# Window attention ahead of two MoE layers: finer steps in the attention's order of issue (key loads apart from query loads, the two shifted copies of the values apart, the softmax of a unit in two halves)

## The chip, the cores and the metric

The kernel runs on one core of a Trainium2 chip. The core has TensorE (PE in the profile; its weight loads are PEld), VectorE (DVE), ScalarE (ACT), GpSimd (POOL) and SyncE (SP), which issues the DMAs of this kernel. Each engine takes its instructions in the order in which the program gives them. The metric is the device time of the one launch, in microseconds.

## The reference

For 4 batches and 8 heads of width 64 there are 512 local tokens and 32 global ones. A local query sees the 32 global keys and the local keys within 32 positions; a global query sees all 544. The result, 2,176 tokens of 512 numbers, goes through two MoE-like layers.

```
s_g = scale * q_g @ k_all.T;  out_g = softmax(s_g) @ v_all
s_ll = where(|i - j| <= 32, scale * q_l @ k_l.T, -1e9)
s_lg = scale * q_l @ k_g.T
out_l = softmax([s_lg, s_ll]) @ [v_g, v_l]
x = concat([out_g, out_l]) as (2176, 512)
h = x @ w1_in;  x = (h * tanh(softplus(h))) @ w1_out
h = x @ w2_in;  y = (h * cos(h)) @ w2_out
```

## The kernel before

The launch has two parts. In the first the attention runs, interleaved with the first work of the first layer; in the second the two layers run, bound by matrix products whose operands are split into a high and a low half.

The attention is cut into 16 pairs of heads (4 a batch) and 32 units, two to a pair. The string ORDER holds all its steps in the order in which they are written into the program, as `name:number`, with an ending `a` or `d` where a copy may go to ScalarE or to VectorE. A step is one Python function that emits instructions for one engine or several. Since every engine is in order, ORDER fixes each engine's own queue, and the DMA queue of SyncE too; how the engines stand against each other is left to the waits. ORDER2 does the same for the second layer.

For a pair `pp`: `lq` loads queries and keys (four DMAs of 128 KB, `qn` and `kn`, two buffers each), `Q` and `K` transpose them on TensorE (L525, L539), `q`, `k`, `k2`, `h` copy them to `QT` and to the windowed keys `kw`, `kg` adds the global keys. For each unit `u`, `S` makes 16 score products (L563) in two of three PSUM buffers `s`; `X` masks and finds the maximum of each of four blocks on VectorE (L579) and exponentiates each on ScalarE (L582); `ne` (POOL, L587), `ni` (DVE), `N` (POOL, L595) normalise; `TA` transposes the probabilities (L606) and `ta` copies them; `NB`, `TB`, `tb` do so for the global keys' part. `lv` loads the values twice, shifted by 32 tokens down (`ve`) and up (`vo`), three buffers each; `lw` overwrites a few rows of `ve` with the global values, so it waits for `lv`'s landing; `vg` loads the global values of a batch. `AV` is the product with the values (L627, L633), `av` its copy into `xT`. The global queries go by pairs of pairs: `lg`, `G`, `g` prepare them, `SG` scores, `sm`, `st`, `se` (an exponential on ScalarE that reads an `s` buffer), `ss`, `si`, `sn` make the softmax, `TG`, `tg` transpose and copy, `AG` and `ag` make and copy the product (L705, L709). PSUM tiles of the transposes and of `AG` and `L` rotate through three buffers.

Between them stand the first layer's steps: `c0` loads 512 KB of weights into one of two buffers `cs` (L209), `c1` and `c5` (ScalarE) and `c2`, `d2`, `c3`, `d3`, `e3`, `c4`, `d5` (VectorE) turn one unit of double-precision weights into a high and a low half, for units 0 to 8; `xs` splits a piece of `xT`, `L` is a first-layer product of 12 matmuls (L795 to L797), `lh` copies it. `ff:0` and `ff:1` run the first group of the second part ahead. After ORDER's last step the second part goes on with the weight conversion, at one or two units a group of products, and with the products themselves (L795 to L797, L1118).

Of the kernel before, what the change touches and what calls it, by code (L numbers as in the profile page):

```python
# [32 lines left out]
    sn:0d N:2 S:4 Q:3 q:3a lv:0 tb:0d kg:3 X:4 TG:0 ni:3 lw:0 S:5 tg:0d TA:2 ne:4 lq:4 AG:0 NB:1 SG:1 X:5 S:6 d2:0  # L33
    ta:2d vg:0 lv:1 c1:0 sm:1 st:1 ag:0 se:1 N:3 ne:5 ni:4 c3:0 TA:3 ni:5 K:4 TB:1 AV:0 ta:3a X:6 ss:1 lw:1 d3:0
    e3:0 G:1 k2:4a N:4 ne:6 k:4d h:4d NB:2 tb:1a S:7 lv:2 si:1 N:5 av:0d AG:1 xs:0a AV:1 lq:5 g:1 TA:4 ni:6 X:7
    c4:0 Q:4 ta:4a ag:1 Q:5 av:1d q:4a N:6 ne:7 K:5 q:5a TA:5 sn:1a ni:7 k:5d kg:4 k2:5d TA:6 ta:5a S:8 c0:1 h:5d
    ta:6a TB:2 N:7 c2:1 tb:2a NB:3 lg:2 TA:7 TB:3 lw:2 G:2 c5:0 ta:7a X:8 S:9 lq:6 tb:3d TG:1 g:2 kg:5 X:9 tg:1d
    SG:2 AV:2 S:10 Q:6 lq:7 ne:8 K:6 sm:2 st:2 ne:9 lv:3 av:2d c1:1 se:2 ni:8 ni:9 NB:4 K:7 X:10 lw:3 S:11 k:6a
    k:7a k2:6d lq:8 ss:2 q:6d lv:4 d2:1 si:2 h:6a k2:7d N:8 kg:6 AV:3 h:7a AG:2 AG:3 ne:10 TA:8 vg:1 X:11 ag:2
    sn:2d ta:8a ag:3 Q:7 lw:4 c3:1 TG:2 q:7a lq:9 S:12 TB:4 N:9 xs:1d d3:1 ni:10 kg:7 xs:2a tg:2d ne:11 lv:5 tb:4a  # L40
    TA:9 av:3d ta:9a K:8 lw:5 X:12 SG:3 e3:1 S:13 N:10 k:8d ne:12 ni:11 k2:8a AG:4 NB:5 AV:4 sm:3 st:3 se:3 X:13
    N:11 ag:4 S:14 h:8d TB:5 av:4d TA:10 ni:12 TA:11 ss:3 ta:10a tb:5d si:3 ta:11a kg:8 Q:8 q:8a K:9 lv:6 X:14 N:12
    ne:13 TA:12 ni:13 S:15 c4:1 NB:6 ta:12d k2:9d k:9a AV:5 h:9a lq:10 lw:6 N:13 AG:5 TB:6 kg:9 X:15 TA:13 ne:14
    av:5d tb:6a ni:14 S:16 lg:3 sn:3d lv:7 ag:5 ne:15 ni:15 ta:13a X:16 TG:3 Q:9 S:17 tg:3d q:9d NB:7 N:14 TA:14
# [86 lines left out]
def kernel(  # L131
# [14 lines left out]
    nc = tc.nc  # L146
# [1103 lines left out]
```

## Time and profile before

| | us |
|---|---|
| median of 3 runs (lowest, highest) | 885.45 (883.87, 886.25) |
| profiled execution: time of its own | 883.55 |
| its span, first to last instruction | 881.8 |
| TensorE busy, of the span | 860.8 (98%) |
| VectorE busy | 738.2 (84%) |
| ScalarE busy | 483.3 (55%) |
| start of the first second-part product (L1118) | 163.76 |

Times in rows are from the span's start. A matmul's shown duration overlaps with the next one's, so TensorE's work is read from the distance between starts, not from durations.

### The profile page before, as it was taken

What the parts mean: (1) busy time and instruction counts of PE and PEld (TensorE: products, weight loads), DVE (VectorE), ACT (ScalarE), POOL (GpSimd) and SP (SyncE); (2) the same over time, 40 slices, a digit from 0 to 9 for tenths busy, and PEclk for the clock granted to TensorE, in tenths of its full rate; (3) what the DMA queues carried; (4) which work ended last, traced back from release to release, by engine and by line L of the source; (5) the groups of instructions that cost most, each with busy time, mean ns of one, the idle gap of its engine ahead of it and who ended that gap; (6) DMA issues with size and microseconds to landing.
All of it is one profiled execution on the core that took longest, in us unless ns stands there. A gap on an engine that the chain in (4) does not pass through costs nothing.

```text
span 881.8 us, 16128 instructions
## 1 busy us (share of the span) xinstructions
PE 860.8 (98%) x5995; PEld 790.4 (90%) x5995; DVE 738.2 (84%) x1513; ACT 483.3 (55%) x948; POOL 85.9 (10%) x137
## 2 busy tenths in 40 slices
PE   7999999999998999999999999999999999999998
PEld 5677888999998999999999998899888888889886
DVE  5989888798889889999989589889776777787786
ACT  6878875674564334444344347566455554545554
POOL 3565565000000000000000000000000000000000
PEclk9999999999999999999999999999999999999999
DMA  7977762156677899887765995724648209025011
GB/s 161 198 158 161 168 152 74 49 156 215 233 252 266 328 338 361 286 294 237 277 243 193 387 414 220 283 90 148 234 144 321 109 14 355 1 79 202 1 60 72
DMA packets 133886, 174.98 MB, mean 198 GB/s; under 512 B 77872, under 2 KB 100400, under 8 KB 133808
## 3 DMA queue, kind: packets, MB, share of 16 engines
q1 hardware_dynamic: 133808, 173.95, 59.8%
q8 instruction: 48, 0.79, 0.4%
q14 instruction: 30, 0.25, 0.1%
HBM read 115.59 MB, written 58.33 MB: 197 GB/s over the span
## 4 chain that ended last, share of the span: by engine, by line
PE 76%; DMA 10%; DVE 8%; ACT 3%; issue 2%; SPq 0%; POOL 0%; DVEq 0%; ACTq 0%; POOLq 0%
PE acc L1019 17%; PE acc L1118 14%; PE h L1050 13%; PE acc L1050 7%; PE h L795 5%; PE h L797 5%; PE h L796 5%; DMA cs<-in_moe_w_out_dram 4%; DMA cs<-in_moe_w_in_dram 2%; PE s L563 2%; PE av L633 1%; DVE ca L237 1%; DMA op<-stage 1%; PE ta L606 1%; DVE x L772 1%
## 5 line engine op out<-in xcount | busy, mean ns | idle before, releaser
L1118 PE MATMUL acc<-gh,w 128*128 128x384 f32 (+1 forms) x768 | 187.9, 328 | 0.0
L1118 PEld LDWEIGHTS acc<-gh,w 128*128 128x128 f32 x768 | 136.2, 189 | 0.0
L1118 PE MATMUL acc<-gl,w 128*128 128x384 f32 (+1 forms) x384 | 126.2, 329 | 2.9 <-DVE x L868 1.9
L795 PE MATMUL h<-x,w 128*128 128x384 f32 (+1 forms) x384 | 126.1, 328 | 0.6 <-DVE x L772 0.5
L797 PE MATMUL h<-x,w 128*128 128x384 f32 (+1 forms) x384 | 125.2, 326 | 0.0
L796 PE MATMUL h<-x,w 128*128 128x384 f32 (+1 forms) x384 | 125.1, 326 | 0.0
L1050 PE MATMUL h<-w,gh 128*128 128x512 f32 x352 | 109.8, 393 | 0.0
L1019 PE MATMUL acc<-xo,w 128*128 128x384 f32 (+1 forms) x402 | 76.4, 327 | 1.6 <-DVE hs L1041 1.6
L1050 PEld LDWEIGHTS h<-w,gh 128*128 128x128 f32 x352 | 66.1, 188 | 11.8
L1118 PEld LDWEIGHTS acc<-gl,w 128*128 128x128 f32 x384 | 72.6, 189 | 4.2 <-DVE x L868 2.2
L1019 PEld LDWEIGHTS acc<-xo,w 128*128 128x128 f32 x402 | 68.0, 188 | 6.6 <-DVE hs L1041 2.8
L841 ACT ACTIVATE w<-w 128x768 f32<-128x768 f32 (+2 forms) x50 | 39.0, 780 | 63.5 <-DVE w L838 63.5
L795 PEld LDWEIGHTS h<-x,w 128*128 128x128 f32 x384 | 72.1, 188 | 1.5 <-issue 0.8
L796 PEld LDWEIGHTS h<-x,w 128*128 128x128 f32 x384 | 72.1, 188 | 0.0
L797 PEld LDWEIGHTS h<-x,w 128*128 128x128 f32 x384 | 72.1, 188 | 0.0
L1050 PE MATMUL h<-w,gl 128*128 128x512 f32 x176 | 69.2, 393 | 2.2 <-DVE part L345 1.0
L1041 DVE TENSOR_TENSOR hs<-u,acc 128x384 f32<-128x384 f32 (+1 forms) x91 | 47.4, 526 | 28.3 <-PE acc L1019 26.9
L831 ACT ACTIVATE k<-hs,magic 128x768 f32<-128x768 f32 (+2 forms) x50 | 43.5, 871 | 49.2 <-DVE w L838 43.1
L1050 PE MATMUL acc<-w,gh 128*128 128x512 f32 x192 | 59.9, 393 | 0.0
L582 ACT ACTIVATE pr<-pr,nm 128x160 f32<-128x160 f32 x128 | 53.2, 421 | 10.6 <-DVE nm L579 10.4
L835 DVE SCALAR_TENSOR_TENSOR w<-k,hs 128x768 f32<-128x768 f32 (+2 forms) x50 | 44.0, 881 | 8.2 <-ACT k L832 6.5
L822 DVE TENSOR_TENSOR gl<-w,gh 128x768 fp32r<-128x768 f32 (+1 forms) x48 | 43.5, 907 | 8.3 <-ACT gh L818 8.3
(179 smaller groups left out, 1783.0 us busy)
## 6 DMA issues: line engine op xcount, KB each, us to landing
w<-scr SPq DMA_DIRECT2D x44, 512.0 KB, 7.0
scr<-co SPq DMA_DIRECT2D x31, 512.0 KB, 3.0
x<-x SPq DMA_DIRECT2D x32, 384.0 KB, 5.9
xo<-op SPq DMA_DIRECT2D x15, 768.0 KB, 5.7
cs<-in_moe_w_in_dram SPq DMA_DIRECT2D x22, 512.0 KB, 4.2
cs<-in_moe_w_out_dram SPq DMA_DIRECT2D x22, 512.0 KB, 4.1
scr<-lab SPq DMA_DIRECT2D x21, 512.0 KB, 3.8
xo<-op SPq DMA_DIRECT2D x10, 640.0 KB, 4.9
```

What stands on the lines that cost most here:

```text
L582: nc.scalar.activation(out=pr[:, i], in_=pr[:, i], func=AF.Exp, bias=nm[:, i:i + 1], scale=-1.0, accum_out=l[:, i:i + 1])
L795: nc.tensor.matmul(ps[:, c, 0:n], wh[:, k, :], xl, start=(k == 0), stop=False)
L796: nc.tensor.matmul(ps[:, c, 0:n], wh[:, k, :], xh, start=False, stop=False)
L797: nc.tensor.matmul(ps[:, c, 0:n], wl[:, k, :], xh, start=False, stop=(k == NK - 1))
L822: nc.vector.tensor_tensor(out=gl, in0=v["w"], in1=gh.bitcast(F32), op=ALU.subtract)
L831: nc.scalar.activation(out=k[:, y], in_=of("h")[:, z], func=AF.Identity, scale=INV2PI, bias=magic[:, 0:1])
L835: nc.vector.scalar_tensor_tensor(out=of("t")[:, z], in0=k[:, y], scalar=-C1, in1=of("h")[:, z], op0=ALU.mult, op1=ALU.add)
L841: nc.scalar.activation(out=of("t")[:, z], in_=of("t")[:, z], func=AF.Sin, scale=0.5)
L1019: nc.tensor.matmul(to, l[:, i + c], r, start=c == 0 and m == 0, stop=c == 1 and m == 2)
L1041: nc.vector.tensor_tensor(out=of[out](), in0=of[x](), in1=bank(s, o), op=ALU.add)
L1050: nc.tensor.matmul(singles()[a], l[:, a * P:(a + 1) * P], r, start=(j, c) == (0, 0) and m == 0, stop=(j, c) == (3, 1) and m == 2)
L1118: nc.tensor.matmul(o[:, 0:n], w[:, a * P:(a + 1) * P], r[:, c, :], start=(not goes_on and g == 0 and m == 0), stop=(not stays and g == G - ...
```

## The change

ORDER is replaced by another sequence of 798 steps in place of 722, and some steps are cut in two so that the parts can stand apart in it:

- `lq` loads queries alone and a new `lk` loads keys;
- `lv` loads `ve` alone and a new `lo` loads `vo`;
- `X` handles the first two of a unit's four blocks and a new `Y` the last two;
- `g` copies the global keys, and a new `gz` the global queries; `tg` copies four blocks, and a new `tu` the fifth;
- the copies of `g`, `gz`, `tu` and `ag`, which VectorE always made, can now go to either engine.

The matrix products, the DMAs with their sizes, the softmax instructions and the conversion steps are the same in number and shape. The 32 units, 16 pairs and 9 loads `c0` all stay; ORDER2 stays as it is.

```
 ORDER = """
-    hot:-1 hot:19 lq:0 K:0 lg:0 k:0a Q:0 q:0a k2:0d h:0a G:0 g:0 lq:1 setup lq:2 lg:1 kg:0 S:0 X:0 Q:1 c0:0 K:1
-    k2:1d k:1d h:1a kg:1 S:1 q:1a Q:2 ne:0 X:1 S:2 ne:1 ni:0 q:2a X:2 K:2 c2:0 SG:0 k:2a lq:3 N:0 ni:1 k2:2a sm:0
-    TA:0 S:3 NB:0 N:1 st:0 ta:0a se:0 h:2d K:3 ne:2 ni:2 TB:0 k:3a X:3 TA:1 k2:3d kg:2 ss:0 si:0 ne:3 h:3d ta:1a
...
+    hot:-1 hot:19 lk:0 K:0 lg:0 G:0 k:0a k2:0d lq:0 Q:0 setup lk:1 g:0d h:0d lq:1 kg:0 q:0a lk:2 K:1 k:1a k2:1a
+    h:1a S:0 lg:1 gz:0d X:0 Y:0 Q:1 q:1d S:1 X:1 kg:1 lk:3 Y:1 SG:0 K:2 ne:0 ni:0 sm:0 S:2 N:0 st:0 k2:2a se:0 lq:2
+    X:2 ne:1 ni:1 k:2d TA:0 N:1 K:3 lv:0 ss:0 Y:2 ta:0d S:3 lq:3 k2:3a h:2d si:0 sn:0d Q:2 TA:1 k:3a h:3a X:3 Q:3
+    q:2d lo:0 G:1 ta:1a kg:2 ne:2 ni:2 NB:0 N:2 gz:1a Y:3 ne:3 S:4 q:3d TB:0 tb:0a lv:1 TA:2 kg:3 g:1d lk:4 X:4 Y:4
...
+    vg:2 N:20 TA:19 TG:4 c0:5 ta:19a tg:4a Y:21 c3:4 c2:5 S:22 SG:5 X:22 tu:4d AV:8 lk:12 Y:22 ne:21 AG:8 ni:21
...
+    ag:11a ni:26 d2:6 Y:27 lv:13 S:28 TB:12 tb:12d av:11a c3:6 ne:27 TA:24 TA:25 ta:24a ni:27 kg:15 lw:12 vg:3 N:26
+    lq:15 c5:5 lv:14 ta:25a lo:13 TG:6 X:28 tg:6a xs:10a xs:11d tu:6d d5:5 AV:12 Y:28 SG:7 S:29 d3:6 sm:7 Q:15
+    av:12a st:7 c0:7 L:8 se:7 lh:8a ne:28 X:29 c2:7 L:9 q:15d e3:6 L:10 ss:7 c1:7 d2:7 lh:9d Y:29 NB:13 ni:28 c4:6
...
+    ta:29d AV:14 c0:9 ni:30 c4:7 TG:7 N:30 lh:13a ne:31 ni:31 c5:7 tg:7a d5:6 L:14 ff:1 NB:15 av:14d c2:8 d5:7 N:31
+    L:15 tu:7d TB:15 lh:14a TA:30 tb:15d lh:15a ta:30d TA:31 AG:14 ta:31d ag:14a AV:15 d2:8 av:15d AG:15 ag:15d
 """
-        def load_qk(pp):
+        def load_tokens(pp, n, src):
             b, p = divmod(pp, NPAIR)
-            qk[pp] = []
-            for n, src in (("qn", q_l), ("kn", k_l)):
-                t = ap.tile([P, NJ, 2, D], F32, tag=n, name=n, bufs=2)
-                for h in range(2):
-                    nc.sync.dma_start(out=t[:, :, h, :], in_=src[b, 2 * p + h].rearrange("(c p) d -> p c d", p=P))
-                qk[pp].append(t)
+            t = ap.tile([P, NJ, 2, D], F32, tag=n, name=n, bufs=2)
+            for h in range(2):
+                nc.sync.dma_start(out=t[:, :, h, :], in_=src[b, 2 * p + h].rearrange("(c p) d -> p c d", p=P))
+            return t
...
+        def load_e(pp):
+            load_v(pp, ve, -32)
+
+        def load_o(pp):
+            load_v(pp, vo, 32)
...
+        def g_copy2(b):
             t, z = live["g", b], qz[b % 2]
-            nc.vector.tensor_copy(out=z[0:64, :, 0:SG], in_=t[0:64, :, 0:SG])
-            nc.vector.tensor_copy(out=z[64:128, :, SG:2 * SG], in_=t[64:128, :, 0:SG])
+            copy("gz", b, z[0:64, :, 0:SG], t[0:64, :, 0:SG])
+            copy("gz", b, z[64:128, :, SG:2 * SG], t[64:128, :, 0:SG])
...
-        def s_max(u):
+        def s_max(u, which=(0, 1)):
...
-            for i in range(4):
+            for i in which:
...
+        def tg_copy2(m):
+            copy("tu", m, pg_of(m)[:, NJ], live["tg", m][1])
...
-            nc.vector.tensor_copy(out=xT[:, p, b * S:b * S + SG], in_=live["ag", pp])
+            copy("ag", pp, xT[:, p, b * S:b * S + SG], live["ag", pp])
```

## Rows read from the trace of the kernel before

**Rows 1.** All engines in order of time, where the second part begins.

```profile
163.52 0.85 ACT L818 ACTIVATE gh<-hraw 128x768 fp32r<-128x768 f32 x1 [2.10 <-PE avg L705]
163.76 0.44 PE L1118 MATMUL acc<-gl,w 128*128 128x384 f32 x1 [0.33 <-DVE xT L709]
```

**Rows 2.** The chain that ended last: start, length, what; three of its later pieces.

```profile
167.73 3.64 DMA cs<-in_moe_w_in_dram
...
272.83 6.02 PE acc L1118 x24
...
283.01 4.16 PE acc L1118 x24
```

**Rows 3.** TensorE's wait at 273 us, and a stretch behind it.

```profile
272.83 0.48 PE L1118 MATMUL acc<-gl,w 128*128 128x384 f32 x1 [1.92 <-DVE x L868]
274.00:276.00 2.00, 2.00 (x8) 2.00 (x8) 2.00 (x4) 2.00 (x4) 0.00 (x0) 0.50 1.02 409
```

**Rows 4.** The same chain: one piece for each kind of attention step.

```profile
53.23 0.70 PE s L563 x16
...
54.31 0.44 PE ta L606 x4
...
55.54 0.89 PE sg L650 x4
...
63.97 0.63 PE av L627 x4
64.60 1.08 PE av L633 x32
65.68 0.56 PE avg L705 x20
```

**Rows 5.** Stretches: length, busy PE, PEld, DVE, ACT, POOL (count), clock, DMA.

```profile
20.00:30.00 10.00, 9.34 (x141) 6.35 (x139) 9.89 (x43) 9.63 (x42) 5.33 (x9) 1.00 0.57 129
```

**Rows 6.** All engines in order of time, the head.

```profile
8.12 0.29 DVE L518 COPY qz<-gt 64x128 f32<-64x128 f32 x1
...
9.20 0.77 PE L563 MATMUL s<-kw,QT 64*64 64x160 f32 x16 [1.47 <-DVE kw L534]
...
13.01 0.17 DVE L591 RECIPROCAL r<-l 128x4 f32<-128x4 f32 x1
...
14.75 0.22 POOL L587 TENSOR_SCALAR l<-l 128x4 f32<-128x4 f32 x1 [2.18 <-ACT pr L582]
...
16.41 0.66 PE L606 MATMUL ta<-ident,pr 128*128 128x128 f32 x4 [0.55 <-POOL pr L595]
...
18.86 0.63 PE L539 MATMUL kt<-ident,kn 128*128 128x128 f32 x4 [1.09 <-DMA kn<-in_k_l_dram]
```

**Rows 7.** Groups by line and shape up to 200 us: busy, mean ns, idle before.

```profile
L513 PE MATMUL gt<-ident,gq 64*128 64x64 f32 x16 | 1.8, 233 | 0.4 <-DMA gq<-in_k_g_dram 0.4
...
L755 ACT COPY PA<-ta 128x512 f32<-128x512 f32 x25 | 14.2, 582 | 1.4 <-PE ta L606 1.2
...
L757 DVE COPY kw<-kt 128x384 f32<-128x384 f32 x16 | 8.5, 551 | 10.8 <-ACT kw L755 10.3 <-PE kt L539 0.5
...
L757 DVE COPY PA<-ta 128x512 f32<-128x512 f32 x7 | 4.8, 679 | 1.2 <-PE ta L606 1.2
...
L709 DVE COPY xT<-avg 128x32 f32<-128x32 f32 x16 | 2.9, 182 | 0.7 <-PE avg L705 0.7
...
L755 ACT COPY kw<-kt 128x192 f32<-128x192 f32 x7 | 2.3, 323 | 2.1 <-DVE kw L757 2.1
```

**Rows 8.** The same chain: copies behind exponentials.

```profile
45.43 1.76 ACT pr L582 x8
```

**Rows 9.** ScalarE and TensorE in order of time, around 127 us.

```profile
126.94 0.69 ACT L213 ACTIVATE ca<-cs 128x512 f32<-128x512 f32 x1 [1.59 <-DMA cs<-in_moe_w_out_dram]
...
128.56 0.66 PE L687 MATMUL tg<-ident,sg 128*128 128x128 f32 x4 [1.06 <-ACT PA L755]
```

**Rows 10.** The line of the weight loads (L209), up to 200 us.

```profile
DMA to landing us min/median/max: 3.4/3.8/6.3
```

More of the change, by code (lines that the diff above doesn't have):

```diff
@@ L457, in attention @@
         NU = 2 * NP
-        gq, kG, QT, pm, PA, PB, av, avt, pg, qk, live = ({} for _ in range(11))
+        gq, kG, QT, pm, PA, PB, av, avt, pg, qn, kn, live = ({} for _ in range(12))
         def load_g(b):
@@ L480, in attention, with load_v @@
         tokens = v_l.rearrange("b h (c p) d -> p (b h c) d", p=P)
-        def load_v(pp):
-            b, p = divmod(pp, NPAIR)
-            E, O = ve[pp % 3], vo[pp % 3]
-            for t, shift in ((E, -32), (O, 32)):
-                t = t.rearrange("p h m d -> p (h m) d")
-                at = 2 * pp * NJ
-                if shift < 0 and pp == 0:
-                    nc.sync.dma_start(out=t[32:P], in_=tokens[0:P - 32, 0:2 * NJ])
-                    nc.sync.dma_start(out=t[0:32, 1:2 * NJ], in_=tokens[P - 32:P, 0:2 * NJ - 1])
-                elif shift > 0 and pp == NP - 1:
-                    nc.sync.dma_start(out=t[0:P - 32], in_=tokens[32:P, at:at + 2 * NJ])
-                    nc.sync.dma_start(out=t[P - 32:P, 0:2 * NJ - 1], in_=tokens[0:32, at + 1:at + 2 * NJ])
-                else:
-                    nc.sync.dma_start(out=t, in_=bass.AP(tensor=tokens.tensor, offset=tokens[:, at].offset + shift * D,
-                                                         ap=[[D, P], [P * D, 2 * NJ], [1, D]]))
+        def load_v(pp, v, shift):
+            t = v[pp % 3].rearrange("p h m d -> p (h m) d")
+            at = 2 * pp * NJ
+            if shift < 0 and pp == 0:
+                nc.sync.dma_start(out=t[32:P], in_=tokens[0:P - 32, 0:2 * NJ])
+                nc.sync.dma_start(out=t[0:32, 1:2 * NJ], in_=tokens[P - 32:P, 0:2 * NJ - 1])
+            elif shift > 0 and pp == NP - 1:
+                nc.sync.dma_start(out=t[0:P - 32], in_=tokens[32:P, at:at + 2 * NJ])
+                nc.sync.dma_start(out=t[P - 32:P, 0:2 * NJ - 1], in_=tokens[0:32, at + 1:at + 2 * NJ])
+            else:
+                nc.sync.dma_start(out=t, in_=bass.AP(tensor=tokens.tensor, offset=tokens[:, at].offset + shift * D,
+                                                     ap=[[D, P], [P * D, 2 * NJ], [1, D]]))
+        def load_e(pp):
+            load_v(pp, ve, -32)
+        def load_o(pp):
+            load_v(pp, vo, 32)
         def load_w(pp):
@@ L524, in q_pe @@
             for j in range(NJ):
-                nc.tensor.transpose(t[:, j, :], qk[pp][0][:, j], ident)
+                nc.tensor.transpose(t[:, j, :], qn[pp][:, j], ident)
         def q_copy(pp):
@@ L538, in k_pe @@
             for j in range(NJ):
[L539 removed]
+                nc.tensor.transpose(t[:, j, :], kn[pp][:, j], ident)
         def k_copy(pp, j=1):
@@ L567, in s_pe @@
                         start=True, stop=True)
-        def s_max(u):
+        def s_max(u, which=(0, 1)):
             jj, s = u % 2, live["s", u]
-            if u % 2 == 0:
+            if ("pr", u // 2) not in live:
                 live["pr", u // 2] = ap.tile([P, 2, 4, W], F32, tag="pr", name="pr", bufs=2)
@@ L574, in s_max @@
             pr = pm[u] = live["pr", u // 2][:, jj]
-            nm, l = [ap.tile([P, 4], F32, tag=n, name=n, bufs=3) for n in ("nm", "l")]
-            live["n", u] = nm, l, live["r", u // 2][:, jj]
-            for i in range(4):
+            if ("n", u) not in live:
+                live["n", u] = *[ap.tile([P, 4], F32, tag=n, name=n, bufs=3) for n in ("nm", "l")], live["r", u // 2][:, jj]
+            nm, l, _ = live["n", u]
+            for i in which:
                 jl, h = divmod(i, 2)
@@ L690, in tg_pe, with pg_of @@
             live["tg", m] = t, t1
+        def pg_of(m):
+            if m not in pg:
+                pg[m] = ap.tile([P, NJ + 1, P], F32, tag="PG", name="PG", bufs=1)
+            return pg[m]
         def tg_copy(m):
-            t, t1 = live["tg", m]
-            a = pg[m] = ap.tile([P, NJ + 1, P], F32, tag="PG", name="PG", bufs=1)
-            copy("tg", m, a[:, 0:NJ], t)
-            nc.vector.tensor_copy(out=a[:, NJ], in_=t1)
+            copy("tg", m, pg_of(m)[:, 0:NJ], live["tg", m][0])
+        def tg_copy2(m):
+            copy("tu", m, pg_of(m)[:, NJ], live["tg", m][1])
         def ag_pe(pp):
```

73 lines of the change are left out of this document (36 added, 37 removed).

## The prediction

> **What bounds the kernel now.** I read the windows of 10 us first, then the chain that ended last, then TensorE in order of time, and last the waits of the attention.
>
> The change touches the first part alone, so the first question is what the second part will make of an earlier start. The second part's products begin at 163.76 us [rows 1]; 718.0 us of the span of 881.8 lie behind that. The chain runs from there to 272.83 through weight loads and VectorE's conversion, with no piece of TensorE's, and from 272.83 through TensorE's products to the end [rows 2]. Its first link is the second group's high half on ScalarE, which waited 2.10 us for the attention's last product [rows 1]. So conversion and products both hang on the attention's end. ORDER leaves the same conversion steps done at that point in both versions (units 0 to 7 whole, unit 8 up to `d2`, the load of unit 9 issued). What the attention saves, the end should therefore get, one for one.
>
> How much is there to save? TensorE's own work between the first scores at 9.20 [rows 6] and 163.76, at the distances of [rows 4]: 32 `S` at 0.70 make 22.4; 332 transposes at 0.44/4 make 36.5; 16 `AV` at 0.63 + 1.08 make 27.4; 16 `AG` at 0.56 make 9.0; 8 `SG` at 0.89 make 7.1; 192 first-layer matmuls at 4.16/24 = 0.173 [rows 2] make 33.2. That is 135.6 of 154.6 us. So TensorE is the fullest engine, and some 19 us at most are waits and changes of kind. In the crowded head VectorE and ScalarE are as full: 9.89 and 9.63 of 10 us between 20 and 30 [rows 5]. They are what TensorE waits for there, so not much of the 19 us can go.
>
> **The change part by part.**
>
> The start. Before the first scores VectorE made two `qz` copies (0.29 us for one [rows 6], the same for its twin) ahead of `kG` and `kw`, for which the scores waited. These move behind, as `gz`; `h:0` comes from ScalarE to VectorE instead, 192 columns, 0.3 us by the 0.323 of ScalarE [rows 7]. 0.58 - 0.3: the scores are 0.3 us earlier. The first queries now stand third in place of first among SP's pairs of DMAs; they are needed only after the keys. Bounds: 0 to 0.6 saved.
>
> The next ten microseconds. From the first `S` to the fifth, 10.9 us passed. Two waits are shown there. `TA:0` waited 0.55 us for `N:0` on GpSimd; its reciprocal had been done at 13.18, but `N:0` stood behind `ne:1`, which waited until 14.75 for the exponentials of unit 1 [rows 6]. In the new order `N:0` stands ahead of `ne:1`. `K:2` waited 1.09 us for its keys [rows 6]: its load stood behind queries, and a 512 KB weight load came close after. Now `lk:2` stands third among the key loads and `c0:0` some 100 steps later. Both waits would go, 1.64. What is late next is `S:3`, whose PSUM buffer is freed by the exponential `se:0`, behind `k2:2` on ScalarE. I take 1.4; bounds 0.4 (the buffers decide) to 2.5 (a share of the rest of that stretch goes too).
>
> The third group of global keys, G:2, waited 0.4 us for its load [rows 7]; `lg:2` is now issued some 11 us of TensorE's work ahead of `G:2` where it was under one. I take 0.4; bounds 0 and 0.4.
>
> The weight load of unit 7. `c1:7` on ScalarE directly followed `c0:7` in ORDER, and waited 1.59 us; behind it on ScalarE stood a split, a probability copy and others, and TensorE lost 1.06 us [rows 9]. Now about 6 us of TensorE's work (`L:8` to `L:10` for the most part) lie between the two. 1.1 saved; bounds 0 to 1.1.
>
> The halves. `X` put four maxima on VectorE and four exponentials on ScalarE in one block of 1.76 us. In four places of the chain a copy that TensorE needed stood behind such a block [rows 8] (three more pieces of the chain are like it). With two maxima and two exponentials at a time, a copy set between waits 0.88 us less: four times 0.88 = 3.5 at most. As the same work has still to be done in a stretch where both engines are full [rows 5], I take 1.0; bounds 0 and 3.5. The instructions stay the same in number, so cutting itself costs nothing.
>
> Copies that change engine. The large ones: 8 `ta` go to VectorE (+8 x 0.679 = 5.4), 11 `k` and `k2` leave it (-11 x 0.551 = 6.1), 9 `ag` leave (-9 x 0.182 = 1.6), and 3 `av` leave (at the 0.679 of the like-sized `ta`, -2.0). ScalarE loses 8 x 0.582 = 4.7 and gains the others. The small ones (`lh`, `xs`, `tb`, `q` to VectorE, `h`, `sn`, `tg`, `tu`, `gz` away) bring VectorE some 1.6 back. VectorE ends 2.7 us lighter, ScalarE about 3 heavier. No row shows the 32-column `ag` copy on ScalarE; it is between 0.16 (0.182 at the ratio 582/679) and 0.323 (192 columns [rows 7]), nearer to the lower by its size, 0.2, so nine of them 1.8, with ends 1.4 and 2.9. VectorE has the more work and is the fuller of the two [rows 5]; the exchange is worth between +3 (ScalarE becomes the bound) and -2.7; I put it at nothing, because either engine's copies lie beside TensorE's products from 60 us on, and if that cover is gone the two ends are what it costs. [...]
>
> New waits. `c2:5` and `c2:7` on VectorE now follow their loads `c0:5` and `c0:7` closely (none and 2 us of TensorE's work between; 6 and 7 before). A load takes 3.4 to 6.3 us to land [rows 10]. SP can run ahead of the other engines, but stands behind `vg`, which waits for a product. Behind `c2` on VectorE stand the maxima of the next scores, for which TensorE's `S` waits. I take 0.4; bounds 0 and 7.6 (below). First-layer products stand more often alone between attention steps (`L:0` to `L:5`, where two stood alone); at one more change of kind each I take 0.4; bounds 0 and 0.7.
>
> Sum: -0.3 - 1.4 - 0.4 - 1.1 - 1.0 + 0.4 + 0.4 = -3.4. The attention ends near 160.4. The profiled execution took 883.55 us (span 881.8 and 1.75 around it), so one like it would take 880.15. That execution lies 1.9 us under the median of the runs, 885.45; on the median the forecast is 882.0.
>
> **The rivals.**
>
> Given back. The waits are only moved: VectorE and ScalarE were nearly full until 60 us, and what TensorE does not wait for at one step it waits for at the next. For it speaks that their work is the same to within 3 us [rows 5]; against it that the waits at 18.86 and 128.56 are a DMA's [rows 6, 9], not work. The start's 0.3 and unit 7's 1.1 would remain, less 0.8 of new waits: -0.6, on the median 884.8, no change that a measurement can tell (0.3%, 2.7 us, is about its limit).
>
> [...]
>
> Slower. VectorE blocks at `c2:5` and `c2:7` for a whole landing, 3.8 us [rows 10], because SP is late with the load. TensorE has `S` and `SG` left, 0.70 + 0.89 [rows 4], about 1.9 with the changes, and then pauses 1.9 us, as at 272.83, and as there works 1.86 us longer at the lower clock: 3.8 for each place, 7.6 for both, in place of the 0.4: 882.0 - 0.4 + 7.6 = 889.2. It decides where SP's lead over VectorE falls under 2 us. For it: at 126.94 such a load did come 1.59 us late [rows 9]. Against: for `c2:5` SP's last wait before is for `AG:6`, some 8 us of TensorE's work earlier, by the distances summed above. [...]
>
> **How the numbers follow.** The forecast, with a range of its own from 879 to 883.5, gets 0.44; the wait less in the second part 0.13; given back 0.28; slower 0.15. The forecast lies 0.4% under the median, on the faster side of 0.3% (882.8), as does the wait less: faster 0.57. No change is the second case, 0.28, and slower 0.15. The range reaches down past the wait less, with the halves and the exchange near their better ends (another 2 us), to 876, and up to where one of the two blocked places costs its full 3.8 on top of no gain, 887.5; that leaves about 2 in 10 outside.
>
> **What would show it.** The first product of L1118 near 160.4 in place of 163.76, and as much behind it as before, 718 us. The first scores near 8.9. No wait of `K:2` or `TA:0` over 0.5 us before 17 us; no wait of ScalarE's L213 over 1 us near 125. Blocks of L582 of half the length in the chain. I am wrong if VectorE's L218 waits for `cs` before 160 us by more than 1 us, if ScalarE becomes the fullest engine between 20 and 100 us, or if the stretch behind the attention is longer or shorter than 718 us by over 2.

## The result and the profile after

The changed kernel took 875.59 us (median of 5 runs, 873.19 to 876.56) against 885.33 for the kernel before (5 runs beside it, 883.87 to 886.25). The ratio is 0.989, 95% interval 0.9873 to 0.9906: 9.7 us faster where 3.4 were forecast, just below the range. The profiled execution took 875.59 us, its span 873.8.

The place where the second part begins, in order of time, after the change:

```profile
155.91 0.41 PE L1133 MATMUL acc<-gl,w 128*128 128x384 f32 x1 [0.43 <-DVE xT L772]
```

163.76 [rows 1] has become 155.91, so the attention ends 7.85 us earlier; behind it lie 873.8 - 155.91 = 717.9 us where there were 718.0. The second part was handed the gain one for one. Even its wait is the same; the same wait in order of time, then a window behind it (length, busy PE, PEld, DVE, ACT, POOL, clock, DMA):

```profile
265.37 0.44 PE L1133 MATMUL acc<-gl,w 128*128 128x384 f32 x1 [1.93 <-DVE x L883]
```

```profile
266.00:270.00 4.00, 4.00 (x16) 4.00 (x16) 4.00 (x9) 3.30 (x6) 0.00 (x0) 0.57 0.85 328
```

TensorE waits 1.93 us for VectorE's addition (1.92 before [rows 3]) and behind it the granted clock is 0.57 for four microseconds (0.50 for two before [rows 3]).

Where the 7.85 us came from is best read from TensorE alone. I took the distance from each of its attention steps to the next and subtracted what that kind of step takes when nothing is waited for (the distances of [rows 4], and the like for the kinds not shown there). What is left over sums to 17.2 us before and 9.3 after:

| stretch | before | after | gain | forecast |
|---|---|---|---|---|
| 0 to 20 us | 6.05 | 4.20 | 1.85 | 1.7 |
| 20 to 60 | 6.06 | 2.13 | 3.93 | 1.4 |
| 60 to 120 | 2.66 | 1.99 | 0.67 | -0.8 |
| 120 to the end | 2.38 | 1.00 | 1.38 | 1.1 |

(In the forecast column the halves and G:2 stand in the second line, the new waits in the third.) More than half of the gap between forecast and result (2.5 of 4.4 us) lies between 20 and 60 us. TensorE's waits in the whole attention, listed by what ended them (us in total, times, longest), before:

```profile
PE s L563 <- DVE kw L534: 1.5, 1, 1.5
PE heat L715 <- POOL ident masks.py:199: 1.4, 1, 1.4
PE kt L539 <- DMA kn<-in_k_l_dram: 1.1, 1, 1.1
PE tg L687 <- ACT PA L755: 1.1, 1, 1.1
PE ta L606 <- POOL pr L595: 0.7, 2, 0.6
PE s L563 <- POOL l L587: 0.7, 1, 0.7
...
PE gt L513 <- DMA gq<-in_k_g_dram: 0.4, 1, 0.4
```

and after:

```profile
PE heat L730 <- POOL ident masks.py:199: 1.3, 1, 1.3
PE kt L548 <- DVE kw L772: 0.4, 1, 0.4
PE acc L1133 <- DVE xT L772: 0.4, 1, 0.4
PE kt L548 <- ACT sg L678: 0.4, 1, 0.4
```

Apart from that of `heat` at the start, 1.35 us, no wait longer than 0.44 us is left. The head, after:

```profile
8.74 0.78 PE L572 MATMUL s<-kw,QT 64*64 64x160 f32 x16
...
12.69 1.04 POOL L605 TENSOR_TENSOR pr<-pr,r 128x512 f32<-128x512 f32 x1 [0.57 <-DVE r L601]
...
13.82 0.22 POOL L597 TENSOR_SCALAR l<-l 128x4 f32<-128x4 f32 x1
...
13.89 0.66 PE L616 MATMUL ta<-ident,pr 128*128 128x128 f32 x4
...
14.94 0.66 PE L548 MATMUL kt<-ident,kn 128*128 128x128 f32 x4 [0.39 <-ACT sg L678]
```

The scores start at 8.74 in place of 9.20; `N:0` (L605, 12.69) now stands ahead of `ne:1` (L597, 13.82), and `TA:0` (13.89) no longer waits; `K:3` at 14.94 waits 0.39 us for ScalarE and for no DMA. These are the steps of [rows 6] without the two waits that the prediction named. Around 127 us, VectorE and TensorE after:

```profile
127.13 0.43 DVE L221 TENSOR_SCALAR ct<-cs 128x512 int32<-128x512 int32 x1 [1.61 <-DMA cs<-in_moe_w_out_dram]
```

```profile
125.14 0.42 PE L810 MATMUL h<-x,w 128*128 128x384 f32 x1
```

Unit 7's weights still come 1.61 us late, now for VectorE's `c2:7`; but TensorE is at `L:8` to `L:10` from 125.14 on and misses nothing.

Last, windows after, and the middle one before:

```profile
20.00:30.00 10.00, 9.96 (x149) 7.24 (x148) 8.66 (x47) 9.58 (x40) 6.30 (x12) 1.00 0.73 167
20.00:60.00 40.00, 39.90 (x622) 30.56 (x621) 36.24 (x158) 37.96 (x144) 26.32 (x42) 1.00 0.89 190
```

```profile
20.00:60.00 40.00, 37.40 (x590) 27.17 (x592) 36.07 (x150) 32.62 (x121) 21.49 (x35) 1.00 0.80 172
```

ScalarE went from 32.62 to 37.96 us of 40, VectorE from 36.07 to 36.24, and TensorE from 37.40 to 39.90.

### The profile page after: what moved, and what is told of

It is laid out like the page before. It is cut to its first block, busy times and chain, and to the rows that moved or that the text cites. A ratio compares the mean times of both kernels' runs of the same rounds, so it can differ in the third digit from the quotient of the medians.

```text
span 873.8 us, 16116 instructions
## 1 busy us (share of the span) xinstructions
PE 859.3 (98%) x5995; PEld 790.5 (90%) x5995; DVE 731.0 (84%) x1499; ACT 485.4 (56%) x962; POOL 84.3 (10%) x137
## 4 chain that ended last, share of the span: by engine, by line
PE 81%; DMA 8%; DVE 8%; issue 1%; ACT 1%; SPq 0%; DVEq 0%; POOL 0%; POOLq 0%; ACTq 0%
PE acc L1034 17%; PE acc L1133 14%; PE h L1065 13%; PE acc L1065 7%; PE h L810 6%; PE h L812 6%; PE h L811 6%; DMA cs<-in_moe_w_out_dram 3%; DMA cs<-in_moe_w_in_dram 3%; PE s L572 3%; PE av L643 2%; PE ta L616 1%; DVE ca L240 1%; DMA op<-stage 1%; PE av L637 1%
```

## The experiments

All are the kernel after or the kernel before with their steps issued in another order or on another engine, unless said otherwise; ORDER's fragments stand for the whole edit. "Attention" is the start of the second part's first product in the run's profiled execution, and a loss of the attention is against the 155.91 of after; a ratio is to the runs of the kernel before on the same chip. The ratio decides whether an edit costs; the profile shows where. A ratio's interval is some 2 to 3 us wide to either side, that of after reaches from 0.9873 to 0.9906, and an edit whose interval overlaps it is not told from after by the ratio alone. One profile is a single execution: in the run with GpSimd's subtractions below the attention is that of after, unedited, and ended at 155.45, so 0.5 us of a loss can be chance. Ratios and profiles differ by some 2 to 4 us in places, since the profiled execution of before took 883.55 us, while the medians of that kernel beside these runs were 885.0 to 887.6.

**Undoing one part in the new order.** The first run puts each second half `Y` directly behind its `X` (24 of the 32 stood apart from it).

```diff
-X:2 ne:1 ni:1 k:2d TA:0 N:1 K:3 lv:0 ss:0 Y:2
+X:2 Y:2 ne:1 ni:1 k:2d TA:0 N:1 K:3 lv:0 ss:0
```

> The new order with each Y set directly behind its X, so that the softmax of a unit is one block of four maxima and four exponentials again, at the place of the first half. Theory H (the halves carry the gain between 20 and 60 us): the attention ends 3 to 4 us later than the changed kernel's 155.9, at 159 or more, and the time rises by as much, to about 879. Theory O (the order carries it, the cuts little): under 1.5 us later. Theory B (VectorE's lighter queue carries it): under 1 us later.

Measured: 879.94 us, ratio 0.9919 (0.9888 to 0.9951), attention 159.59, a loss of 3.7. The chain between 47 and 75 us has the blocks of eight instructions on ScalarE again:

```profile
50.65 1.75 ACT pr L593 x8
...
59.24 1.76 ACT pr L593 x8
...
64.29 1.65 ACT pr L593 x8
...
68.32 1.76 ACT pr L593 x8
```

The loss lies where these lie, 2.2 us of it between 50 and 70. By the sums of the table above, 0.4 of it falls before 20 us, 1.2 between 20 and 60, all behind 50, 1.7 between 60 and 120 and 0.4 behind: most of what the order gained before 60 us stands without this cut. In this order the cut is worth 3.7 us of the attention, 2.6 by the ratios (0.0029 of 885); the intervals overlap, but all four runs (877.60 to 880.48) lie above the five of after (873.19 to 876.56).

Next, both loads of a pair one behind the other, for queries and keys (15 of 16 pairs) and for the values and their shifted copy.

```diff
-lv:6 h:9a NB:6 ... lo:6 lw:6
+h:9a NB:6 ... lo:6 lv:6 lw:6
```

> The new order with keys and queries of a pair loaded together again (15 of 16 pairs) and the two copies of the values together. H, O and B alike: 0 to 1 us later than 155.9, for the queries ahead of the second keys in the head; a loss over 2 us would mean that SP's finer queue is a cause of its own.

Measured: 879.75 us, ratio 0.9929 (0.99 to 0.9957), attention 160.58, a loss of 4.7; 2.7 of it fell before 20 us. My expectation, at most 1, was wrong. Part of the 2.7 goes with a lower clock: TensorE waited 1.01 and 1.09 us for loads in the first 10 us, the granted clock over the first 20 us was 0.83 (1.00 in after), and 16 score products took 1.35 us at 10.04 and 1.50 at 12.36, but 0.78 at 16.37. The profiled execution, 882.49, was also the longest of the five. Two runs split the loss: queries and keys of the first four pairs alone, and the values alone.

> The kernel after, with queries and keys of the first four pairs loaded directly one behind the other again (the other pairs as in the change, values as in the change). The runs with all loads together lost 4.7 us of the attention, 2.7 of them in the first 20 us. If the head's share is that of the order of these four pairs, this run loses 2 to 3.5 us (median 877.5 to 879), all before 30 us, with waits of first products for DMA. If the loss comes from the loads behind them, it loses under 1.

> The kernel after, with the two loads of values (plain and shifted copy) of every pair directly one behind the other; queries and keys as in the change. If the cut of the values' load matters, this loses 1 to 2.5 us, the part that the run with all loads together lost behind 30 us; if the head's four pairs are the whole of it, the time stays within 0.9 of 875.6.

Measured: 875.64 us (0.9896, 0.9879 to 0.9912), attention 156.50, a loss of 0.6 only; and 880.01 us (0.9946, 0.9927 to 0.9965), attention 159.41, a loss of 3.5. My expectation for the head was wrong: this run issues the same loads in the same order up to 10 us as the run with all loads whole, but its profile has neither of the two DMA waits nor the lower clock (its mean over the execution was 0.998, there 0.994), so that order alone does not bring them. The values' loads count. With the values whole, 11 of the 16 pairs had both loads at the later of their two places, pair 6 among them; two more runs put every whole load at the earlier one (queries and keys too in the second).

```diff
-lv:13 lw:12 vg:3 lq:15 lv:14 lo:13
+lv:13 lo:13 lw:12 vg:3 lq:15 lv:14 lo:14
```

> The kernel after with the two loads of values of every pair directly one behind the other, but at the place of the earlier of the two (the run before had them at the later place and lost 3.5 us of the attention). If the cut itself matters, because the second load is put too early and holds up SyncE's queue, 1.5 to 4 us are lost here too. If only the lateness cost it, under 0.7 is lost, and the cut of this load is worth nothing that an earlier whole load doesn't give.

> The same with queries and keys too (15 of 16 pairs), all at the earlier place. At the later place all loads together lost 4.7 us of the attention, 2.7 of it in the first 20 us. If the loads' cut carries gain, 2 to 5 are lost (877.5 to 880.5); if a load may be whole as long as it is early, under 1 is lost.

Measured: 878.19 us (0.9911, 0.9877 to 0.9944), attention 158.33, 2.4 lost; and 878.70 us (0.9928, 0.9904 to 0.9953), attention 159.59, 3.7 lost. Late, whole values cost beyond noise. Early, the evidence is weaker: both intervals overlap that of after, but with all loads early all seven runs (878.11 to 880.19) lie above those of after, while with the values alone two of six (874.90 and 876.40) lie among them. With the values late, SyncE's queue and TensorE in order of time:

```profile
65.86 2.17 SPq L499 DMA_DIRECT2D ve<-in_v_l_dram  x1
...
71.54 0.33 SPq L510 DMA_DIRECT2D ve<-in_v_g_dram  x1
...
73.45 0.34 PE L643 MATMUL av<-PA,ve 128*64 128x64 f32 x4 [1.62 <-DMA ve<-in_v_g_dram]
```

`lv:6` goes out at 65.86; `lw:6` (L510), which writes into the same buffer, only at 71.54, and `AV:6` waits 1.62 us for it. In the kernel after the two go out at 57.61 and 64.16. With the values early, and the same step in the kernel after:

```profile
119.68 1.81 SPq L485 DMA_DIRECT2D vg<-in_v_g_dram  x4
...
123.20 1.05 PE L637 MATMUL av<-PB,vg 64*128 64x256 f32 x4 [1.11 <-DMA vg<-in_v_g_dram]
```

```profile
117.65 1.94 SPq L485 DMA_DIRECT2D vg<-in_v_g_dram  x4
...
121.15 0.71 PE L637 MATMUL av<-PB,vg 64*128 64x256 f32 x4
```

`lo:13` now stands ahead of `vg:3` (L485), which goes out 2.03 us later (0.87 of it the whole attention is behind by then), and `AV:12` waits 1.11 us for it. As I read it, what the cut of this load gives is that `lv` can be early enough for `lw` while `lo` lets more urgent loads pass.

The third undoing keeps the order and puts 103 copies back on the engine that they had before.

```diff
-gz:1a ... k:5a ... tu:2a
+gz:1d ... k:5d ... tu:2d
```

> The new order and all its cuts, but each copy on the engine that it had in the kernel before (g, gz, tu and ag on VectorE): 103 of the 798 steps change engine. B: VectorE is 2.7 us heavier, the attention ends 2.5 us or more later than 155.9. H and O: 0 to 1.5 us later, mostly in stretches where the order had been searched with the other engine.

Measured: 898.80 us, ratio 1.014 (1.0105 to 1.0175), attention 177.57: 21.7 lost, though VectorE was busy only 6.2 us longer up to the end of the attention and ScalarE 2.2 less. The exponentials by group (busy, mean, idle before them, ended by), with the old engines (up to 160 us) and after:

```profile
L592 ACT ACTIVATE pr<-pr,nm 128x160 f32<-128x160 f32 x126 | 52.7, 422 | 25.0 <-DVE nm L589 24.9
```

```profile
L592 ACT ACTIVATE pr<-pr,nm 128x160 f32<-128x160 f32 x128 | 53.5, 423 | 8.8 <-DVE nm L589 8.0
```

ScalarE stands 24.9 us waiting for VectorE's maxima in place of 8.0. So the sum of either engine does not tell the cost; that it is set by which copy stands in front of which maximum is my reading of these waits.

The fourth undoes all five cuts (halves, loads, `gz`, `tu`, and `ag` on VectorE) and keeps the new sequence.

> The new order with all five cuts undone: halves together, loads together, gz behind g, tu behind tg, and gz, tu, ag on VectorE as before. What is left of the change is the sequence alone. H: at least 5 of the 8 us are lost, the attention ends at 161 or later. O: at most 3 are lost, it ends before 159, and the kernel stays at least 5 us faster than the one before.

```diff
-gz:1a Y:3 ne:3 ... tu:0d ... ag:0a
+Y:3 (behind X:3) ... gz:1d (behind g:1d) ... tu:0d (behind tg:0d) ... ag:0d
```

Measured: 883.95 us, ratio 0.9961 (0.9937 to 0.9984), attention 163.55. In the profile 7.6 of the 7.85 us are gone, by the ratios 6.3 of 9.7. The sequence with the engines of its other copies, which one theory had as the cause, carries about a third by the ratios. Of the 7.6, 2.7 lie before 20 us, where TensorE waited 1.29 us for `kn` and the granted clock was lower too (0.91 over these 20 us). Between 20 and 60 us, 2.0 of the 3.9 us gained are still there.

**Doing one part in the old order.** First the cutting alone: the old order in the new steps, with nothing between the pieces.

```diff
-lq:0 ... X:0 ... g:0
+lq:0 lk:0 ... X:0 Y:0 ... gz:0d g:0d
```

> The order and the engines of the kernel before, written in the new finer steps with nothing moved between the pieces: the cutting alone. The prediction had it that cutting itself costs nothing: within 1 us of the kernel before. Its profile is also a second look at the old order, of whose executions the first profile was one of the quickest: if the old order has waits that come in some executions only (for the load of pair 5 near 35 us, in two of the kernels built on it), the attention here ends 1 to 4 us later than 163.76, with the difference at few places; if not, within 0.5 of it.

Measured: 883.99 us (0.9988, 0.9967 to 1.001), attention 163.86: the cutting alone brings and costs nothing, as forecast. Then, each in a run of its own: `c0:7` to the place behind `e3:5`; the first four pairs' loads keys first; 16 of the 32 second halves behind the next copy; and the new engines for the 103 copies.

```diff
+e3:5 c0:7 ag:11
...
+lk:0 K:0 lg:0 lq:0 ... lk:1 lq:1 setup lk:2 lq:2 lg:1 ... K:1 lk:3 lq:3 c0:0
...
+X:u (copy) Y:u
...
-gz:1d ... k:5d ... tu:2d
+gz:1a ... k:5a ... tu:2a
```

> The kernel before with one step moved: the load c0:7 directly behind e3:5, ahead of vg:3 and lw:13. The wait of 1.59 us on ScalarE near 126 and TensorE's 1.06 us behind it should go: the attention ends 1.0 to 1.6 us earlier, at 162.2 to 162.8. If the wait is only moved (rival 'given back'), under 0.4 earlier.

> The old sequence with the loads of the first four pairs set as keys ahead of queries, the first global load ahead of the first queries, and the 512 KB load c0:0 behind the fourth pair's loads. If the separate key loads carry the head (the whole-loads run lost 2.7 us before 20 us): the fifth S starts 1.5 to 2.5 us earlier than 20.07 and the attention ends as much earlier. If the head is held by VectorE and ScalarE: the wait of the fourth K (1.09 us) goes, but the end moves by under 1 us.

> The old sequence with 16 of the 32 second halves Y set behind the next copy, the others directly behind X. Theory H in its plain form (a copy between the halves waits less, whatever the order): 1 to 2 us earlier than 163.76. Theory J (halves, engines and order only gain together, as one searched sequence): between 1 us earlier and 2 us later.

> The old sequence, uncut, with the 103 copies on the engines that the new order gives them, which makes VectorE 2.7 us lighter and ScalarE about 3 heavier. Theory B (balance): the attention ends 1 to 2.7 us earlier than 163.76. Theory J (which engine takes a copy is right only for the place in the sequence): it ends 5 us or more later, as the new order with the old engines did (21.7 us later).

| run | median | ratio (95%) | attention |
|---|---|---|---|
| unit 7's load earlier | 883.43 | 0.9974 (0.9951 to 0.9997) | 163.88 |
| head's loads | 887.04 | 1.0005 (0.9991 to 1.0019) | 167.69 |
| halves | 887.46 | 1.002 (1.0 to 1.0041) | 169.30 |
| engines | 899.10 | 1.0147 (1.0129 to 1.0165) | 178.84 |

Only unit 7's load gains by itself, and barely beyond noise (2.3 us by the ratio, 0.3 at the near end of the interval). Its wait is gone from the profile, but the attention ended no earlier: TensorE stood 1.44 us at `K:5` (36.76 us), where it did not wait in the profile of before. The other three gain nothing or lose; the engines cost 15 us of the attention here. The run of the halves is no clean test of what the prediction priced, copies behind ScalarE's exponentials: 12 of its 16 copies are VectorE's in the old order.

The run of the head's loads does not test their order. TensorE lost 3.95 us at `K:3`, and the trace names no releaser, but in order of time the cause shows:

```profile
20.41 0.43 DVE L221 TENSOR_SCALAR ct<-cs 128x512 int32<-128x512 int32 x1 [4.53 <-DMA cs<-in_moe_w_in_dram]
...
21.76 0.35 DVE L772 COPY kw<-kt 128x192 f32<-128x192 f32 x1
...
22.21 0.68 PE L548 MATMUL kt<-ident,kn 128*128 128x128 f32 x4 [3.95 <-issue]
```

The edit moved the load `c0:0` back (it goes out at 13.93 us, where before it went out at 10.47) and left its first reader, `c2:0` on VectorE, in its place. VectorE stood 4.53 us for the load with its other work behind it, and `K:3` began 0.10 us after a copy of that work had ended. It is the mechanism of the prediction's rival "slower", brought about by the edit.

**Moving the halves by one copy.** To see whether the cut or its place carries the 3.7 us, 14 second halves went one copy later, and in another run 13 of them one copy earlier.

```diff
-X:25 N:23 L:5 lo:11 Y:25 N:24 lh:5d
+X:25 N:23 L:5 lo:11 N:24 lh:5d Y:25
...
-X:22 tu:4d AV:8 lk:12 Y:22
+X:22 Y:22 tu:4d AV:8 lk:12
```

> The kernel after, the halves still cut, but 14 of the second halves issued one copy later than the order has them. If the cut as such carries the 3.7 us that undoing it cost, this keeps most of it and loses under 1.5 (median under 877). If the gain hangs on the place that the order gives each second half, so that nearly any other place costs as much as no cut, this loses 2.5 to 6 (878 to 882).

> The kernel after with 13 of the second halves issued one copy earlier than the order has them (the halves still cut; the run before had 14 of them one copy later and lost 5.2 us of the attention). If the place is what counts, this loses 2 to 5 too (877.5 to 881). If later is worse only because the probabilities come later, this loses under 1 or gains.

Measured: later, 879.15 us (0.9938, 0.9922 to 0.9954), attention 161.10, 5.2 lost (4.2 by the ratios), at least as much as with no cut at all; earlier, 876.99 us (0.9891, 0.9857 to 0.9925), attention 156.33, 0.4 lost. So not every place is as bad as no cut, as I had it for the other case: one copy earlier costs nothing that can be told from noise, one copy later does. One of the places, with the halves later:

```profile
108.71 0.43 ACT L592 ACTIVATE pr<-pr,nm 128x160 f32<-128x160 f32 x1 [1.25 <-DVE nm L589]
...
110.06 0.57 ACT L770 COPY PA<-ta 128x512 f32<-128x512 f32 x1
...
110.68 0.43 PE L658 MATMUL sg<-kw,qz 128*64 128x32 f32 x8 [1.16 <-ACT PA L770]
```

ScalarE first waits 1.25 us for maxima that VectorE now makes later, its probability copy (L770) follows at 110.06, and `SG` waits 1.16 for that copy. This second half, pushed back, delays what stands behind it on two engines.

**Splicing the two orders** at the scores of unit 15 (near 57 us): the new order first and the steps left over in the old, then the reverse.

```diff
-... S:15 (then on in the new order)
+... S:15 (then all steps left, in the old order and on the old engines)
```

> The order of the kernel after up to the scores of unit 15 (near 57 us), and behind it all steps that remain in the order and on the engines of the kernel before. TensorE's excess over its own work fell by 5.8 us up to 60 us (12.1 to 6.3) and by 2.1 behind it. If what a stretch gains stays gained, as the profile of the second part suggests, this kernel keeps 5.8 and loses 2.1: the attention ends near 158, the median is 877 to 878.5. If the gain hangs on the sequence as a whole, so that a seam costs like any other departure from it, 2 to 5 more are lost: 879.5 to 883. If it is given back, it stands within 1 of the kernel before.

> The reverse: all steps of the kernel before up to the scores of unit 15, with its engines, then the rest in the order and on the engines of the kernel after. If stretches add up, it gains only the 2.1 of behind 60 us: the attention ends near 161.7, the median is 882 to 884. If a seam costs, it is no faster than the kernel before, 885 to 889. If the gain of the first 60 us were only waits put off in the kernel after, the whole 7.9 would show here, 876 to 878.

Measured: 882.82 us (0.996, 0.9935 to 0.9984), attention 160.41; and 884.64 us (0.9994, 0.9967 to 1.002), attention 166.05. Up to 50 us the first has 5.7 us of TensorE's excess, where after has 6.0 and before 10.7: the new order's gain is there by then and is not asked back. It then loses at the seam (2.9 us of excess between 50 and 60, where after has 0.4 and before 1.5) and at unit 7's load, which is the old one's wait, and longer:

```profile
123.62 0.66 ACT L216 ACTIVATE ca<-cs 128x512 f32<-128x512 f32 x1 [2.65 <-DMA cs<-in_moe_w_out_dram]
...
125.22 0.66 PE L697 MATMUL tg<-ident,sg 128*128 128x128 f32 x4 [2.13 <-ACT PA L770]
```

The reverse has the head of before, loses at its seam too (an excess of 2.4 between 60 and 80 us; 1.1 before, 0.9 after) and wins 1.1 behind. It also shows a wait that the old order has in some executions only, for the load of pair 5:

```profile
36.14 0.63 PE L535 MATMUL qt<-ident,qn 128*128 128x128 f32 x4 [1.58 <-DMA qn<-in_q_l_dram]
```

The same step waited 1.49 us with the halves in the old order and the next one 1.3 in the cutting alone, each for a DMA, and 1.44 with unit 7's load moved, where the trace names ScalarE; in the profile of before none did. In the reverse and with the halves the granted clock was 0.96 over 20 to 60 us, where before had 1.00. Of the new order's profiles only that with all cuts undone waits for this pair, 0.48 us at `K:5`.

**A step beyond the change.** The 1.93 us at 265 us wait for VectorE, which has 1.96 us of low-half subtractions in front. Those of the second part, 24 in the trace, go to GpSimd.

```diff
-                x_chunk(src, n, k, i, pool, nc.scalar, nc.vector, x, ("x", t0, k))
+                x_chunk(src, n, k, i, pool, nc.scalar, nc.gpsimd, x, ("x", t0, k))
```

> The kernel after, with one edit outside the change: in the second part the 20 subtractions that make the low halves of the tokens' columns run on GpSimd (16 like-sized ones of the attention took 1.04 us each there) in place of VectorE (0.49 to 0.55 us each). Four of them, 1.96 us in one block at 258.35, stand ahead of the addition that came 1.93 to 2.3 us late for TensorE at 263 and behind which the clock fell. If that pause comes from VectorE's backlog, as the prediction's rival of a wait less in the second part has it, the stretch behind the attention goes from 717.9 to 714 to 716 and the median falls by 2 to 4 us, to 872 to 874; the attention stays at 155.9. If the backlog comes from the loads of the weights, which VectorE also waits for there, or GpSimd's slower operations are late for the products, the stretch stays within 1 of 717.9 or gets longer.

Measured: 884.63 us (0.9991, 0.9977 to 1.0004), attention 155.45, but 725.5 us behind it: 7.6 lost. VectorE, GpSimd and TensorE around the place:

```profile
259.45 4.94 POOL L787 TENSOR_TENSOR x<-xT,x 128x384 fp32r<-128x384 f32 x4 [11.99 <-ACT x L784]
...
259.69 1.51 DVE L337 TENSOR_TENSOR co<-ct,co 128x512 fp32r<-128x512 f32 x1
...
261.13 1.23 DVE L236 TENSOR_SCALAR ca<-ct 128x512 int32<-128x512 int32 x1
...
262.28 1.24 DVE L221 TENSOR_SCALAR ct<-cs 128x512 int32<-128x512 int32 x1
...
263.44 1.50 DVE L240 SCALAR_TENSOR_TENSOR ca<-cs,ca 128x512 f32<-128x512 uint32 x1
...
267.54 0.68 DVE L337 TENSOR_TENSOR co<-ct,co 128x512 fp32r<-128x512 f32 x1
268.14 0.41 DVE L236 TENSOR_SCALAR ca<-ct 128x512 int32<-128x512 int32 x1
...
271.77 0.69 PE L1133 MATMUL acc<-gl,w 128*128 128x384 f32 x1 [3.92 <-DVE x L883]
```

The pause became 3.92 us, 2.0 more; other pauses of the second part, up to 2.2 us for VectorE's `gl`, add to the 7.6. While GpSimd worked, VectorE's instructions took 1.50 and 1.23 us in place of 0.68 and 0.41 behind it: the four slow ones alone cost some 3.3 us, more than the 1.96 of which VectorE was to be relieved.

No run beat the changed kernel.

## Why the prediction was wrong

**What bounds the kernel** was read rightly: all of the gain is in the attention, TensorE was the fullest engine there, and the 718 us behind moved as one block.

**The start and the next ten microseconds** were right: 1.7 forecast, 1.85 measured, with both waits of [rows 6] gone. The wait at 18.86 there was that of `K:3`, whose load stood behind `c0:0`, and not of `K:2`; the reason given, a load in a queue, was the right one. What the order of these loads is worth by itself stays open: with these pairs whole in the new order 0.6 was lost, about what one profile can tell, and the run in the old order lost its time at another load.

**Unit 7's load** was right: 1.1 forecast, some 1.4 measured at its stretch; the load is still late, and the cover of `L:8` to `L:10` is what took the wait from TensorE. It is the one part that gained alone, if barely beyond noise.

**The halves**, and the argument by which I priced them, are the step that failed. I put a bound of 3.5 on them and took 1.0, "as the same work has still to be done in a stretch where both engines are full". That rested on one window of ten microseconds [rows 5]. Over 20 to 60 us before, VectorE was busy 36.07 and ScalarE 32.62 of 40: nearly full in one window is not full in the stretch. The same work fitted in with 2.5 us more of TensorE's, so what TensorE waited for there was in good part the order of the instructions in the queues. The stretch gained 3.9 where the halves and `G:2` were given 1.4; undoing the cut costs 3.7 of the attention (2.6 by the ratios), about the upper bound. The place was not as forecast either: undoing it costs 1.2 between 20 and 60 us and 2.1 behind, and with all five cuts undone the stretch still keeps 2.0 of its 3.9. So the argument failed for the whole order and not for the halves alone: "not much of the 19 us can go" took VectorE and ScalarE for a ceiling that the stretch did not have. (The 19 were even too many: `SG` was taken at 0.89, the second of its two groups of products, where the step takes 1.25, so eight of them leave 2.9 less.) The rival that this argument fed, "given back", is refuted by the result, where no stretch lost what another had gained; in the splice, 3.3 of the 5.0 us gained by 50 us were left at the attention's end, and the rest went at the seam and at unit 7's load.

**The loads of the values** were not costed at all. Put back together they cost 3.5 us of the attention late, with a wait for `lw`, and 2.4 early, with a wait for `vg`; the second is not clear of noise.

**The exchange of engines** was put at nothing from the engines' sums. The sums themselves missed something: VectorE's busy time up to the attention's end fell by 7.5 us (129.97 to 122.50) where 2.7 were forecast, and 5.6 of it come from three kinds of conversion instruction that stayed on VectorE and ran shorter (the last section has them). The `ag` copies on ScalarE, taken at 0.2, measured 0.185 us each. And the term was no sum: in the old order the new engines lose 15 us of the attention, in the new order the old ones lose 21.7, with the busy time different by a few. Parts costed one by one against the old order do not add up here: undone singly, halves, loads (late) and engines cost 3.7 + 4.7 + 21.7 = 30.1 us of an attention that gained 7.85 (by the ratios 28.2 of 9.7), and of those done singly in the old order only the move of unit 7's load brought anything. So the gain belongs to order, cuts and engines fitted to one another; the sum of separate terms against the old order was the wrong form for it.

**The new waits** (0.8) did not come. VectorE did stand 1.61 us for weights at 127 us, as I had called a sign of being wrong, but the first-layer products beside it covered it, and the "slower" rival's pause of TensorE never opened. The 1.86 us that this rival adds for each pause are the 6.02 - 4.16 us of 24 products at one place [rows 2]; no run shows them as the price of every pause of 1.9 us, and behind 1.93 us in the run without halves the clock stayed at 1.00. ScalarE did become fuller than VectorE between 20 and 100 us (73.9 against 70.6 us busy of 80; TensorE 79.9), which comes near my other sign, and it did no harm.

**The second part.** A wait less there, to which 0.13 went, would have been the pause at 273 us gone [rows 3], 1.92 us, with these 1.86 us behind it. The pause came again, 1.93 us long, and 717.9 us lay behind the attention.

**The median.** The forecast carried over the 1.9 us by which the profiled execution of before lay under its median. After, profile and median agree to the hundredth, which makes some 1.8 of the 9.7 and is no part of the span's 8.0. The wait at pair 5, 1.3 to 1.6 us in four profiles of kernels built on the old order and absent in that of before, is a wait of this kind; that it makes up the 1.8 is argued, not shown, and the cutting alone had it and still ended its attention at 163.86.

What stays open: whether a search for an order without the cuts would have found as much. The run without the cuts used the order found with them.

## What to carry to other kernels

Where a kernel's engines are in order and none is full over the whole stretch, cost a new order by the queues: name for each wait of the bounding engine the instruction that stands ahead of what it waits for. A window of ten microseconds in which an engine is full bounds these ten microseconds alone. Don't expect one part of a searched order to bring its share in another order: test the whole, and cut a block or a load where something urgent can then go first, and see what stands behind the second piece. Where you move a load, look for its first reader: left in its old place, it stops its engine (VectorE for 4.53 us here).

## What the runs showed of the hardware

The clock behind a pause of TensorE is not told by the pause's length alone. The same wait of 1.93 us, in the run without halves:

```profile
268.93 0.44 PE L1134 MATMUL acc<-gl,w 128*128 128x384 f32 x1 [1.93 <-DVE x L884]
```

```profile
266.00:270.00 4.00, 2.08 (x12) 1.76 (x11) 4.00 (x9) 1.69 (x5) 0.00 (x0) 1.00 0.73 180
270.00:274.00 4.00, 4.00 (x25) 4.00 (x24) 4.00 (x8) 2.82 (x5) 0.00 (x0) 1.00 0.96 376
```

There the granted clock stayed at 1.00 behind it. It was 1.00 over 274 to 278 us too in the runs with a pause of 1.63 and 1.39 us at this place (up to 275.55 and 276.78; head's loads and halves in the old order, whose second parts were 716.4 and 716.3 us long), while behind 1.90 us in the run with all cuts undone (up to 272.34) it was 0.85 over 270 to 274 us and 0.73 over the next four. In the run with whole loads, where TensorE waited 1.01 and 1.09 us for loads within the first 10 us, the clock granted over the first 20 us was 0.83. The mean granted clock also goes with the time of whole runs: of the 23 runs of the kernel before beside the splices, the ten of 886.80 us and more had 0.993 to 0.996, the others 0.995 to 1.000.

VectorE's instructions took longer beside GpSimd's in the run with GpSimd's subtractions above: 0.68 us became 1.51 (L337), and the same holds for the one-operand L236 and L221 (1.23 and 1.24 us in place of 0.41 and 0.43). GpSimd's four took 1.24 us each where 16 like-sized ones of the attention took 1.04.

VectorE shows the same in the attention, before more than after. One of three kinds of conversion instruction up to the attention's end, before and after (busy, mean ns):

```profile
L218 DVE TENSOR_SCALAR ct<-cs 128x512 int32<-128x512 int32 x9 | 6.2, 694 | 1.3 <-DMA cs<-in_moe_w_in_dram 1.3
```

```profile
L221 DVE TENSOR_SCALAR ct<-cs 128x512 int32<-128x512 int32 x9 | 4.0, 439 | 1.7 <-DMA cs<-in_moe_w_out_dram 1.6
```

With `ca<-ct` (5.6 to 3.7 us) and `ct<-ct,ca` (6.9 to 5.4) the three came from 18.7 us to 13.1 in the same number and shape. Before, those that ran beside an instruction of GpSimd took 0.83, 0.74 and 0.93 us on the mean, the others 0.43, 0.42 and 0.68. What this gave the attention no run shows by itself.
